# An attention, Fourier-mixing and MLP kernel: model-dimension tables from row-shift matmuls, a scale read from PSUM, fold work on GpSimd, and clock-keeping matmuls

## The chip, the cores and the metric

The kernel runs on one core of one Trainium2 chip. The metric is the device time of one execution, in microseconds (us). A time is "of an execution"; a span is the stretch from the first to the last instruction in the profile, about 2 us shorter. Executions of one kernel differ by 1 to 2%, and those more than 1.5% above the fastest of the same kernel are called slow and left out of ratios.

The engines are named as the profile names them: PE is TensorE's matmul, PEld its weight load, DVE is VectorE, ACT is ScalarE, POOL is GpSimd and SP is SyncE. On this kernel SP issues the input loads, and POOL issues the weight loads.

## The reference, cut to what matters

```python
B, H, S, D = 4, 8, 768, 48                    # r, k, v, w: (B, H, S, D); u: (H, D)
for t in range(S):                            # attention with a decaying state
    cur   = k_t^T v_t * u
    y_t   = r_t (state + cur)
    state = w_t * state + k_t^T v_t
x = y.transpose(0, 2, 1, 3).reshape(4, 768, 384)
mixed = real(fft(fft(x, axis=1), axis=2))     # over the sequence, then over the model dimension
u  = x + mixed
un = (u - mean(u)) / sqrt(var(u) + 1e-6)
out = u + relu(un @ w_ch1) @ w_ch2            # (384 x 1536), (1536 x 384)
```

## The kernel before

Every batch passes through three stages. Attention takes 768 tokens as six chunks of 128 and gives `x`. The mix multiplies `x` with cosine and sine tables: first the sequence tables `CS` and `SS`, then the model-dimension tables `DTM` and `DTP`, which gives `uf = x + mixed`. The MLP multiplies with `W1` and `W2`. The kernel computes its tables itself, at the start.

The program is a list of operations. Each names its engine, an estimated duration, what it reads and writes, and a key. A greedy list scheduler in the kernel runs over it once, before launch, and fixes the order on every engine: at each step it takes the operation that can start first, and the one with the lowest key where several can. So nine numbers, from which most keys are made, and the estimated durations decide the order of everything. On the chip each engine then works through its own list in that order.

```python
# --- tables (cut): angles on VectorE, sine on ScalarE
for q in range(NC // 2):                      # 3 sequence tables: 4 VectorE operations each
    ...                                       # TF[q], TG[q]: angles
    sins.append(act(SS[:, q, :], TF[q][:, :], ACTF.Sin, scale=sc))
    sins.append(act(CS[:, q, :], TG[q][:, :], ACTF.Sin, scale=-sc, bias=BHPI[:, :]))
...                                           # 16 one-column operations on VectorE: MC, MN, MSH, MB, CP
for j in range(3):                            # 3 model-dimension tables, again 4 VectorE operations each
    ...
    op("dve", 550, stt(f, ki, MC[:, j:j + 1], q, ALU.mult, ALU.add), ...)
    sins.append(act(DTM[:, j, :], f, ACTF.Sin, scale=sc2, bias=MB[:, j:j + 1]))
op("act", 8000, all_sins, ...)                # one operation for all nine Sins: needs ALL angles
...
# --- weights: 6 loads issued by GpSimd, held back until the third chunk's v has landed
op("pool", 1000, lambda e, q=q: e.dma_start(W1[:, q, :], moe_w_ch1[...]), r=[("in", "v", 2)], ...)
...
# --- attention(b, c): one chunk (cut)
op("act", 500, act(L[:, :, 0:D], wt[:, :, :], ACTF.Ln), ...)                    # lb
op("act", 470, act_ps(e1, tce), r=[tce], w=[("E1", i2)])                        # exp, PSUM -> SBUF
op("pool", 1050, tt(rk[:, :, :], rt[:, :, :], kt[:, :, :], ALU.mult), ...)
op("act", 500, act(vb[:, :, :], vt[:, :, :], ACTF.Copy), ...)                   # vb: v in bf16
op("dve", 700, tt(rh[:, :, 0:D], rt[:, :, :], e1[:, :, :], ALU.mult), ...)      # rh = r * exp
...                                           # transposes, rtb, ktb, masked products ah, state, y
op("dve", 530, ...)                                                             # x = y + vtd
op("dve", 350, tt(xf[:, c, 64:256],  xb[:, c, 0:192], xb[:, c, 384:192:-1], ALU.add), ...)       # even fold
op("dve", 350, tt(xf[:, c, 256:447], xb[:, c, 1:192], xb[:, c, 383:192:-1], ALU.subtract), ...)  # odd fold
# --- mix(b) (cut)
op("act", 475, ...)                                                             # hcs, from the sequence transform
op("dve", 390, lambda e, j=j: e.tensor_copy(out=hcr[:, j, :], in_=hcs[:, j, S // 2:0:-1]), ...)
...                                           # uf, statistics
op("dve", 100, ts(nmu[:, :], agg[:, kb, 0:1], -1.0, None, ALU.mult), ...)
op("act", 600, act(un[:, :], uf[:, kb, :], ACTF.Identity, bias=nmu[:, :]), ...) # un = u - mean
...                                           # transposes of un; W1: 288 matmuls; W2: 288 matmuls
A0, AP, F0, FL, M0, ML, P, KT, KW = 39.3, 5.6, 23.3, 16.1, 48.9, 42.4, 44.9, 7.9, 13.3
```

## Time and profile before

| | before |
|---|---|
| time, median of 3 (range) | 237.49 us (236.5 to 238.16) |
| span of the profiled run | 235.8 us |
| first W1 matmul | 72.24 us |
| VectorE busy before it | 66.64 of 72.24 us |
| PE busy after it | 156.74 of 163.56 us |

First, the page of the kernel before. The first line is the busy time of each engine with its share of the span. The others cut the span into 40 slices of 5.9 us; each digit is the busy share of one slice in tenths, and `PEclk` is the granted clock of the tensor engine in tenths of full speed.

```profile
PE 200.0 (85%) x1776; PEld 130.1 (55%) x1776; DVE 185.5 (79%) x403; ACT 153.1 (65%) x316; POOL 105.0 (45%) x118
PE   0765475549769999999998999899989999999994
DVE  8999999398998389999769998894899866822222
PEclk9998555577995999999999999999999999999999
DMA  6999999989970559852365678104200000020102
```

Read the rows against each other. In the first twelve slices most of PE's digits are 4 to 7, its clock is at 5 or 7 in six of them, and VectorE and DMA have mostly nines. From then on nearly all of PE's digits are nines. So there are two stages, and the mean share of PE, 85%, describes neither.

The next view is the busy time of each engine in two stretches of the kernel before, cut at the first W1 matmul. The columns are the stretch, its length, then busy time and number of instructions of PE, PEld, DVE, ACT and POOL, then mean granted clock, DMA share and GB/s.

```profile
0.00:72.24 72.24, 43.25 (x362) 27.72 (x363) 66.64 (x149) 42.01 (x79) 47.93 (x60) 0.77 0.99 186
72.24:235.80 163.56, 156.74 (x1416) 102.41 (x1414) 118.88 (x255) 111.12 (x238) 57.09 (x58) 0.99 0.34 80
```

In the first stretch VectorE (66.64 of 72.24) and DMA (share 0.99) are full, and PE is not. In the second, PE is busy 156.74 of 163.56 us.

The chain of waits of the kernel before, followed back from the last instruction, has these pieces among others. The columns are start, length in us, and what it was; L389 is a helper for activations, L620 is `x`, and L708 is W1.

```profile
24.82 16.01 DMA in_v<-in_v_dram
...
40.85 0.52 ACT vb L389
...
57.79 0.47 DVE x L620
...
72.45 0.96 PE bank L708 x3
```

The last chunk's `v` lands at 40.83 us, but the last `x` of batch 0 starts 17 us later, and W1 another 15 us later. What lies between is shown by the timeline of the kernel before (start, length, engine, line, operation, output and inputs):

```profile
38.42 0.60 DVE L383 SCALAR_TENSOR_TENSOR ht<-ki,mc,tq 128x384 f32<-128x384 f32 x1
...
44.88 0.53 ACT L389 ACTIVATE ss<-uf 128x385 bf16<-128x385 f32 x1
...
48.67 0.60 ACT L389 ACTIVATE dtm<-ht,mb 128x384 bf16<-128x384 f32 x1
...
57.72 0.54 DVE L620 TENSOR_TENSOR x<-bank,vtd 128x384 f32<-128x384 f32 x1
...
64.80 1.01 DVE L666 TENSOR_TENSOR uf<-bank,x 128x384 f32<-128x384 f32 x2
```

The first line is the last of the table angles, on VectorE at 38.42 us. The Sins wait for it and for their turn, so they run to 49.3 us.

Next are two of the three forms of `rh` in the kernel before, which differ only in the buffer. The numbers are the shortest, median and longest duration in ns, then the first and last start.

```profile
L375 DVE TENSOR_TENSOR rh<-in_r,e_0 x8: 525/554/1370, 7.1 to 177.0; 128x384 bf16<-128x384 f32 x8
L375 DVE TENSOR_TENSOR rh<-in_r,e_1 x8: 548/1158/1347, 13.7 to 180.4; 128x384 bf16<-128x384 f32 x8
```

The same operation on the same shape takes about 0.55 us or, in ten of all 24, 0.99 to 1.37 us, which is the sign of something that blocks it at times. The trace shows what it is: each of the ten starts while a multiplication on GpSimd is under way, and ends 0.41 to 0.43 us after that one ends. Of the fourteen short ones only two start during one, in its last 0.16 us.

Last, waits of the kernel before in the stretch after the first W1 matmul: who waited for what, us in total, times, longest.

```profile
PEld bank L648 <- DVE xf L375: 2.8, 6, 1.0
...
PE bank L648 <- DVE xf L375: 1.0, 2, 0.6
...
PE bank L612 <- DVE ah L587: 0.9, 1, 0.9
PE bank L564 <- DVE rh L375: 0.9, 1, 0.9
```

### The profile page before, as it was taken

The numbers are of one execution on the slowest core, as the hardware profiler recorded it, in microseconds if no ns is written. First come the engines' busy times: TensorE is split into PE (matmuls) and PEld (weight loads), VectorE is DVE, ScalarE is ACT, GpSimd is POOL, SyncE is SP. The second block draws the span as 40 slices with busy tenths as digits, with TensorE's granted clock in tenths as the row PEclk, the third lists the DMA queues.
The fourth block names the chain that finished last, engine by engine and source line by source line (L and its number), as shares of the span: only waits on it lengthen the run. The fifth ranks groups of instructions, "written<-read, shape, count | busy, mean of one in ns | idle before, by whom it ended". The sixth has DMA issues, their size and how long they took to land.

```text
span 235.8 us, 4671 instructions
## 1 busy us (share of the span) xinstructions
PE 200.0 (85%) x1776; PEld 130.1 (55%) x1776; DVE 185.5 (79%) x403; ACT 153.1 (65%) x316; POOL 105.0 (45%) x118
## 2 busy tenths in 40 slices
PE   0765475549769999999998999899989999999994
PEld 0443253436335575666776766467757765666652
DVE  8999999398998389999769998894899866822222
ACT  3554542997466997566887977488969554965340
POOL 7587894629901589282165965401633100000000
PEclk9998555577995999999999999999999999999999
DMA  6999999989970559852365678104200000020102
GB/s 120 211 213 219 183 189 197 214 176 216 198 143 3 100 104 211 191 117 52 81 155 104 133 156 181 38 0 110 60 0 3 36 33 33 3 101 0 70 33 100
DMA packets 105478, 26.45 MB, mean 112 GB/s; under 512 B 100336, under 2 KB 105072, under 8 KB 105456
## 3 DMA queue, kind: packets, MB, share of 16 engines
q1 hardware_dynamic: 103440, 23.80, 47.5%
q0 software_dynamic: 2016, 2.36, 5.9%
q8 instruction: 14, 0.23, 0.4%
q14 instruction: 8, 0.07, 0.1%
HBM read 23.79 MB, written 4.72 MB: 121 GB/s over the span
## 4 chain that ended last, share of the span: by engine, by line
PE 63%; DVE 19%; DMA 9%; ACT 5%; issue 2%; SPq 1%; DVEq 0%; ACTq 0%
PE bank L727 19%; PE bank L708 18%; DMA in_v<-in_v_dram 7%; DVE xf L375 6%; PE bank L648 6%; PE bank L664 5%; PE bank L564 3%; PE bank L583 3%; DVE rh L375 3%; DVE ah L587 3%; DVE x L620 2%; PE bank L684 2%; DMA in_w<-in_w_dram 2%; PE bank L612 2%; PE bank L570 1%
## 5 line engine op out<-in xcount | busy, mean ns | idle before, releaser
L708 PE MATMUL bank<-unt,w 128*128 128x384 bf16 x288 | 58.0, 333 | 0.0
L727 PE MATMUL bank<-w,ht 128*128 128x384 bf16 x288 | 54.1, 326 | 0.0
L717 ACT ACTIVATE ht<-bank 128x384 bf16<-128x384 f32 x80 | 37.9, 500 | 19.2 <-PE bank L708 19.0
L587 DVE TENSOR_TENSOR ah<-bank,msk 128x512 bf16<-128x512 f32 x48 | 31.1, 679 | 8.2 <-PE bank L583 8.1
L375 POOL TENSOR_TENSOR vtd<-in_v,dc 128x384 f32<-128x384 f32 x24 | 21.1, 884 | 35.8 <-DVE dc L545 32.7
L708 PEld LDWEIGHTS bank<-unt,w 128*128 128x128 bf16 x288 | 26.9, 99 | 16.1 <-issue 1.0
L727 PEld LDWEIGHTS bank<-w,ht 128*128 128x128 bf16 x288 | 26.9, 98 | 15.3
L573 ACT ACTIVATE rtb<-bank 128x1024 bf16<-128x1024 bf16 x24 | 24.6, 1025 | 15.0 <-PE bank L564 14.8
L732 DVE SCALAR_TENSOR_TENSOR osb<-bank,rstd,uf 128x384 f32<-128x384 f32 x24 | 14.8, 615 | 17.2 <-PE bank L727 16.7
L375 DVE TENSOR_TENSOR xf<-x 128x192 bf16<-128x192 f32 (+1 forms) x48 | 26.6, 593 | 0.1
L375 POOL TENSOR_TENSOR rk<-rk,ub 128x384 f32<-128x384 f32 x24 | 25.2, 1051 | 1.3
L375 POOL TENSOR_TENSOR rk<-in_r,in_k 128x384 f32<-128x384 f32 x24 | 25.4, 1060 | 0.0
L564 PE MATMUL bank<-idb,rh 128*128 128x128 bf16 x192 | 17.2, 242 | 8.7 <-DVE rh L375 8.1
L375 POOL TENSOR_TENSOR kh<-in_k,e_0 128x384 bf16<-128x384 f32 x8 | 8.8, 1096 | 31.3 <-ACT e_0 L538 31.3
L575 ACT ACTIVATE ktb<-bank 128x512 bf16<-128x512 bf16 x24 | 14.3, 597 | 9.5 <-PE bank L570 9.3
L564 PEld LDWEIGHTS bank<-idb,rh 128*128 128x128 bf16 x192 | 13.7, 108 | 11.8 <-DVE rh L375 8.5
L612 PE MATMUL bank<-vb,ah 128*128 128x48 bf16 x192 | 15.8, 189 | 5.0 <-DVE ah L587 4.9
L583 PE MATMUL bank<-rtb,ktb 128*128 128x256 bf16 x96 | 17.4, 309 | 1.8 <-ACT rtb L573 1.1
L525 PE MATMUL bank<-lb,msk 128*128 128x384 bf16 x24 | 9.4, 391 | 11.1 <-ACT lb L389 11.1
L713 DVE TENSOR_SCALAR ht<-bank 128x384 bf16<-128x384 f32 x16 | 8.8, 552 | 12.6 <-PE bank L708 12.6
L612 PEld LDWEIGHTS bank<-vb,ah 128*128 128x128 bf16 x192 | 13.1, 100 | 9.5 <-DVE ah L587 6.5
L389 ACT ACTIVATE lb<-in_w 128x384 bf16<-128x384 f32 x24 | 12.5, 523 | 5.9 <-DMA in_w<-in_w_dram 5.9
(111 smaller groups left out, 403.1 us busy)
## 6 DMA issues: line engine op xcount, KB each, us to landing
in_w<-in_w_dram SPq DMA_DIRECT2D x24, 192.0 KB, 3.7
in_k<-in_k_dram SPq DMA_DIRECT2D x24, 192.0 KB, 3.7
in_r<-in_r_dram SPq DMA_DIRECT2D x24, 192.0 KB, 3.7
in_v<-in_v_dram SPq DMA_DIRECT2D x24, 192.0 KB, 3.5
out_dram<-osb SPq DMA_DIRECT2D x24, 192.0 KB, 1.9
w<-in_moe_w_ch_dram POOLq DMA_DIRECT2D x6, 384.0 KB, 9.7
ub<-in_u_dram SPq DMA_DIRECT2D x1, 192.0 KB, 3.8
```

Source lines behind the costliest of these rows:

```text
L375: return lambda e: e.tensor_tensor(out=o, in0=a, in1=b, op=f)
L564: ins = e.transpose(psb(trr)[:, 128 * h:128 * h + 128], rflat[:, o0:o0 + 128], IDB[:, :])
L573: op("act", 1000, lambda e: e.activation(rT[:, :, :].rearrange("p h t -> p (h t)"), psb(trr)[:, :], ACTF.Copy), r=[trr], w=[("RTB", i2)])
L575: op("act", 570, lambda e: e.activation(kT[:, :, :].rearrange("p h t -> p (h t)"), psb(trk)[:, 0:512], ACTF.Copy), r=[trk], w=[("KTB", i2)])
L583: ins = e.matmul(ps(ta)[:, 256 * x:256 * x + 256], kT[:, q, :], rT[:, 2 * q:2 * q + 2, :].rearrange("p h t -> p (h t)"))
L587: op("dve", 660, lambda e, hf=hf, ta=ta: e.tensor_tensor(out=ah[:, 4 * hf:4 * hf + 4, :], in0=ps(ta)[:, :].rearrange("p (h t) -> p h t", t ...
L612: ins = e.matmul(ps(ty)[:, D * h:D * h + D], ah[:, h, :], vb[:, h, :], start=True, stop=first)
L648: return e.matmul(ps(t)[:, 0:HF], xf[:, s, off:off + 128], tab[:, s, :], start=a, stop=z)
L708: ins = e.matmul(ps(t)[:, 0:384], W1[:, m, 128 * j:128 * j + 128], unt[:, m, :], start=(m == 0), stop=(m == NM - 1))
L717: op("act", 475, lambda e, j=j, t=t, ht=ht: e.activation(ht[:, j, :], ps(t)[:, 0:384], ACTF.Relu), r=[t], w=[("HT", q % 2, j)])
L727: ins = e.matmul(ps(t)[:, 0:DM], ht[:, j, 128 * x:128 * x + 128], W2[:, j, :], start=(j == 0), stop=(j == NJ - 1))
L732: op("dve", 540, lambda e, kb=kb, t=t, o=o: e.scalar_tensor_tensor(out=o[:, :], in0=ps(t)[:, 0:DM], scalar=rstd[:, kb:kb + 1], in1=uf[:, k ...
```

## The change

The intent is to take work off VectorE in the first stage, to have the tables early, and to keep the tensor engine's clock up while it is poorly fed.

1. The model-dimension tables are rows of the sequence tables in another order, because 768 is twice 384. 14 small matmuls with shifted identities (`IDW`, `NIDW`) pick these rows out of `CS` and `SS` into PSUM, and ScalarE copies them to `DTM` and `DTP`. Their angles, three Sins and the 16 one-column operations go (two new ones make `CP`).
2. The exponential that scales `r` is written in place in PSUM, and `rh` reads it there.
3. The odd fold of batches 1 to 3 and the reversed copy `hcr` go from VectorE to GpSimd; the `ALT` vector too.
4. `un` becomes mean minus u, and its transposes use the negative identity, so `nmu` goes.
5. 24 pairs of matmuls into a bank that nobody reads are strewn over the first stage, to keep the clock up.
6. All nine numbers of the keys are chosen anew; the tables get first priority (`KT` 0.0).
7. Estimated durations of operations that stay are changed too (the even fold from 350 to 520 ns, `vtd` from 1050 to 890, `osb` from 540 to 610, the angles of the sequence tables), and with them the order.

```diff
-        op("dve", 350, ts(ALT[:, :], TQ[1][:, :], -2.0, 1.0, ALU.mult, ALU.add), ...)     # and 4 before it
+        op("pool", 300, fill(ALT[:, :], 1.0), w=["ALT0"])
+        op("pool", 200, fill(ALT[:, 1::2], -1.0), r=["ALT0"], w=["ALT"])
 ...
-        op("dve", 100, ts(IS1[:, :], p, 62.5, None, ALU.is_gt), ...)                      # and 15 like it
-        for j in range(3):
-            ...                                                                           # 4 VectorE operations
-            sins.append(act(DTM[:, j, :], f, ACTF.Sin, scale=sc2, bias=MB[:, j:j + 1]))
+        for j in range(3):
+            def rows(e, j=j, t=t):
+                for half in range(2):
+                    for i, (cos, q, p0, np_, sh) in enumerate(moves[j]):
+                        tab = (CS if cos else SS)[p0:p0 + np_, q, :]
+                        idn = (IDW if cos or half else NIDW)[p0:p0 + np_, 128 - sh:256 - sh]
+                        src = tab[:, 0:HF:2] if half == 0 else tab[:, HF - 3:0:-2]
+                        ins = e.matmul(dst, idn, src, start=(i == 0), stop=(i == len(moves[j]) - 1))
+            op("pe", 600, rows, ...)
+            op("act", 475, ... e.activation(DTM[:, j, :], ps(t)[:, 0:DM], ACTF.Copy) ...)
+            op("act", 475 + 100, ... e.activation(DTP[:, j, :], ps(t)[:, 0:DM], ACTF.Copy, scale=...) ...)
 ...
-        op("act", 470, act_ps(e1, tce), r=[tce], w=[("E1", i2)])
+        op("act", 470, lambda e: e.activation(ps(tce)[:, 0:DM], ps(tce)[:, 0:DM], ACTF.Exp), w=[tce])
 ...
-        op("dve", 700, tt(rh[:, :, 0:D], rt[:, :, :], e1[:, :, :], ALU.mult), ...)
+        op("dve", 550, lambda e: e.tensor_tensor(out=rh[:, :, 0:D], in0=ps(tce)..., in1=rt[:, :, :], op=ALU.mult), ...)
 ...
-        op("dve", 350, tt(xf[:, c, 256:447], xb[:, c, 1:192], xb[:, c, 383:192:-1], ALU.subtract), ...)
+        op("dve" if b == 0 else "pool", ..., tt(xf[:, c, 256:447], ...), ...)
 ...
-            op("dve", 390, lambda e, j=j: e.tensor_copy(out=hcr[:, j, :], in_=hcs[:, j, S // 2:0:-1]), ...)
+            op("pool", 500, lambda e, j=j: e.tensor_copy(out=hcr[:, j, :], in_=hcs[:, j, S // 2:0:-1]), ...)
 ...
-    A0, AP, F0, FL, M0, ML, P, KT, KW = 39.3, 5.6, 23.3, 16.1, 48.9, 42.4, 44.9, 7.9, 13.3
+    W0, WP, NW = 8.0, 1.6, 24
+    A0, AP, F0, FL, M0, ML, P, KT, KW = 46.4, 4.2, 24.5, 13.8, 48.1, 44.3, 45.6, 0.0, 0.5
 ...
+    for i in range(NW):
+        def warm(e):
+            for x in range(2):
+                ins = e.matmul(ps(tw)[:, 0:384], MSK[:, :], IDW[:, :])
+            return ins
+        o = op("pe", 324, warm, r=["MSK", "IDB"], w=[tw], key=1e6)
+        o.ready0 = 1e3 * (W0 + WP * i)
```

## The prediction

> **What bounds it now.** Two phases. From 72.45 us (first W1 matmul, in the chain of waits) to the end at 235.8 the tensor engine is busy 156.5 of 163.4 us at clock 0.99 (busy time by windows), and the chain runs almost only through its matmuls: PE-bound. Before 72.45 the PE's mean clock is 0.77 and it often waits. There VectorE is the limit: busy without a gap from 0.9 to 41 us (timeline), since tables and attention of batch 0 share it. The Sin calls run only at 43.6-49.3 us, batch 0's last `x` at 57.7, its first `uf` at 64.8. DMA is the other limit: share 1.0 or more from 10 to 50 us at about 200 GB/s; chunk 5's `v` lands at 40.85.
>
> **What the change does.**
> - Removes from VectorE before the first mix: the `alt` chain (2.7 us), about 20 one-column operations (about 3), DTM angles (7.7), DTP (1.6): about 14 us with overlaps taken off (groups by line). Adds about 0.8 for wider identities. 14 row-shift matmuls (0.16-0.2 us each) and six 0.5 us PSUM copies on ScalarE replace three 0.6 us Sins.
> - The table gets first priority: in the instruction order all angles precede the first `ah`, and the Sins follow chunk 2's exponential. I expect Sins at 15-22 us.
> - `rh` reads its scale from PSUM: 24 at mean 0.84 us become about 0.55. Now they are 0.55 unblocked, 1.16-1.37 blocked. The Trainium skill, "SBUF — State Buffer", "Who interferes with whom", says a VectorE instruction with two SBUF inputs contends with a GpSimd one that reads SBUF, and with one it does not; the two clusters agree.
> - Per later batch VectorE loses six odd-half `xf` (0.55), three `hcr` (0.52), six `nmu` (0.14): about 6 us; GpSimd gains as much, to 31 of 45 us. Slack of a PE-bound stage: worth 0-2 us.
> - 48 clock-keeping matmuls, 8-16 us of PE time, all before the first W1 matmul, mostly in idle gaps. They should hold the clock near 1 at 24-60 us, where it is 0.5-0.7 now ("TensorE: Matmul & The Clock Gate", Part 1: the clock falls after an idle window and returns after sustained activity).
>
> **Sum.** From instruction counts times full-clock durations (0.163 us for 384 columns), PE work after the first W1 matmul is 152 us before, 153 after: an estimate. So the time moves by the start of that phase. VectorE's work up to the first `uf`, unblocked, is about 41 us after (about 60 now). DMA still delivers chunk 5 no sooner than 36-41 us; then 5-6 us to `x`, 4-5 to `uf`, 6-7 to W1 (7.6 now, at a reduced clock). First W1 matmul: 57 us (52-63) instead of 72.5. The later phase keeps its 163 us, less 1-2 for a clock that no longer dips (0.70 at 72-80), plus 1 for work moved. 57 + 163 + 1.7 (time above span) = 222 us.
>
> **Right if:** first W1 matmul at 52-63; VectorE has gaps before 41 us, waiting for DMA; Sins before 23 us; `rh` mean 0.55; clock at least 0.9 in 10-60 us; second phase 160-165 us; first-phase DMA share still about 1.
>
> **Wrong if:** the weights, now issued at about 15 us, take bandwidth from chunks 3-5, so batch 0 ends past 50 us; the Sins stall chunks 1-2; GpSimd's odd-half folds queue behind `rk`/`vtd` and starve the mix later; warm matmuls, in order, sit before urgent ones. These push toward 230. Batch 0 flowing at DMA speed pushes toward 214.
>
> Predicted 222 us, range 214-230; faster by over 2%: 0.91, within 2%: 0.07, slower: 0.02.

## The result, and the profile after

In its first four executions the changed kernel took 223.81 us (median; 220.48 to 224.77) against 237.0 (236.3 to 238.16), a ratio of fast runs of 0.9349 [0.9237, 0.946]; two of the four, at 224.75 and 224.77, count as slow. Its profiled execution was a slow one, so the kernel was run and profiled again with five rounds: 223.03 us (220.36 to 223.25, six executions), against 237.15 (235.15 to 237.85) for the kernel before in the same rounds. That ratio is 0.9392 [0.9345, 0.9438], or 6% faster. A ratio is the mean time of one kernel's fast runs over that of the other's in the same rounds, so it is not quite the ratio of the medians that are quoted. The profile below is the one of the repeated run, which was fast; it is used for all comparisons.

> The changed kernel once more, in the rounds that the next kernels share, because its profiled run fell in the slower state. Expected: 218 to 223 us, ratio to before 0.93 to 0.945, first W1 matmul at 62 to 65 us, the stretch after it 156 to 160 us long.

The page of the changed kernel (slices of 5.5 us):

```profile
PE 199.4 (90%) x1838; PEld 130.6 (59%) x1838; DVE 156.6 (71%) x316; ACT 151.4 (69%) x319; POOL 118.7 (54%) x150
PE   0687586989799999999999999999999999999994
DVE  8998955994975797859678976783997839522322
PEclk9999958999969999999999999999999999999999
DMA  5999999999994979951254993015001010111102
```

VectorE has 29 us less work in all, PE's is the same although it has 62 more matmuls, and the clock row has lost its fives but one.

The two stretches of the changed kernel, cut at its first W1 matmul (columns as above):

```profile
0.00:61.65 61.65, 43.65 (x406) 26.95 (x407) 51.98 (x104) 40.60 (x78) 45.66 (x62) 0.94 1.04 195
61.65:220.60 158.95, 155.72 (x1432) 103.67 (x1432) 104.57 (x213) 110.77 (x242) 73.06 (x89) 0.99 0.39 91
```

The first stretch is 10.6 us shorter, and the second 4.6 us. The DMA share of the first has gone up to 1.04, VectorE's load has come down to 51.98 of 61.65 us.

The chain of waits of the changed kernel from 17 to 66 us (L384 is the activation helper, L370 the helper of `xf`, L649 is `uf`, L688 is W1):

```profile
18.70 17.23 DMA in_v<-in_v_dram
...
35.96 0.52 ACT vb L384
...
37.52 2.12 DVE xf L370 x2
...
54.66 1.02 DVE uf L649 x2
...
61.65 0.83 PE bank L688 x3
```

Here the chain again passes a load of `v`, but it is the fifth chunk's and not the last one's. It is issued at 18.70 us, amid the six weight loads that GpSimd issues from 17.2 to 21.2 us, and lands 17.2 us later; the median load of `v` in this run takes 3.6. The last chunk's `v` is issued only at 38.33 us, and lands at 42.01. The same thing was in the kernel before, with the weights issued from 22.6 us on and the last chunk's `v`, issued at 24.82, taking 16.0 us; there VectorE was late anyway. From that landing on, the chain of the changed kernel is VectorE and PE work without a large wait.

The timeline of the changed kernel (the lines of POOL issue the weight loads):

```profile
17.15 1.82 POOL L488 DMA_DIRECT2D w<-in_moe_w_ch_dram  x3
17.20 0.53 ACT L384 ACTIVATE ss<-uf 128x385 bf16<-128x385 f32 x1
...
18.94 2.27 POOL L491 DMA_DIRECT2D w<-in_moe_w_ch_dram  x3
...
19.47 0.60 ACT L384 ACTIVATE cs<-ht,bhpi 128x385 bf16<-128x385 f32 x1
...
49.79 0.56 DVE L606 TENSOR_TENSOR x<-bank,vtd 128x384 f32<-128x384 f32 x1
...
54.66 1.02 DVE L649 TENSOR_TENSOR uf<-bank,x 128x384 f32<-128x384 f32 x2 [2.85 <-PE bank L647]
```

The six remaining Sins are done at 20.1 us instead of 49.3. The last `x` of batch 0 starts at 49.79 instead of 57.72, and `uf` at 54.66 instead of 64.80; before `uf` VectorE is now idle for 2.85 us, where it had no gap before.

`rh` in the changed kernel:

```profile
L538 DVE TENSOR_TENSOR rh<-bank,in_r x24: 538/547/559, 8.5 to 171.1; 128x384 bf16<-128x384 f32 x24
```

All 24 are short. The Trainium skill, "SBUF — State Buffer", section "Who interferes with whom", says that a VectorE instruction with two SBUF inputs contends with a GpSimd one that reads SBUF, and that with one SBUF input it does not; the one that comes second waits in full. The slow ones of 0.99 to 1.37 us, each of which outlasted a GpSimd instruction that had started first, are gone once one input comes from PSUM.

PE's waits in the second stretch of the changed kernel. There are no lines of `PE` any more, only of `PEld`, and these are the two largest:

```profile
PEld bank L688 <- issue: 0.9, 5, 0.3
PEld bank L569 <- ACT ktb L561: 0.6, 2, 0.4
```

### Where the 15.2 us of span come from

From the number and width of the matmuls in a stretch and their durations at full clock (0.163 us for 384 columns, 0.109 for 256, 0.057 for 128, 0.043 for 96, 0.025 for 48), PE's work after the first W1 matmul is an estimate of 152.1 us before and 153.3 after. So the span is start + work + rest:

| | first W1 matmul | PE work after it (estimate) | rest | span |
|---|---|---|---|---|
| before | 72.24 | 152.1 | 11.5 | 235.8 |
| after | 61.65 | 153.3 | 5.65 | 220.6 |
| difference | -10.6 | +1.2 | -5.85 | -15.2 |

The rest falls into PE's idle time, 163.56 - 156.74 = 6.8 us before and 158.95 - 155.72 = 3.2 after, and into busy time above the estimate, 4.6 and 2.4. In the first 7.8 us after the start the clock was 0.70 before and 0.78 after, so some 0.6 us (7.8 x 0.08) of the second part is clock, by estimate; what the other 1.6 us are was not found.

### The profile page after: what moved, and what is told of

Its sections match the earlier page's. It is cut to its first block, busy times and chain, and to the rows that moved or that the text cites. A ratio compares the mean times of both kernels' runs of the same rounds, so it can differ in the third digit from the quotient of the medians.

```text
span 222.5 us, 4731 instructions
## 1 busy us (share of the span) xinstructions
PE 198.4 (89%) x1838; PEld 130.2 (59%) x1838; DVE 157.4 (71%) x316; ACT 151.2 (68%) x319; POOL 118.8 (53%) x150
## 3 DMA queue, kind: packets, MB, share of 16 engines
q0 software_dynamic: 2016, 2.36, 6.3%
## 4 chain that ended last, share of the span: by engine, by line
PE 75%; DMA 8%; SPq 8%; DVE 4%; ACT 3%; issue 1%; DVEq 0%
PE bank L688 22%; PE bank L707 21%; DMA in_v<-in_v_dram 8%; SPq L393 8%; PE bank L631 7%; PE bank L647 4%; PE bank L550 4%; PE bank L569 4%; PE bank L598 2%; PE bank L556 2%; PE bank L664 2%; PE bank L601 2%; PE bank L510 1%; PE bank L512 1%; DVE xf L370 1%; PE bank L586 1%
## 5 line engine op out<-in xcount | busy, mean ns | idle before, releaser
L688 PE MATMUL bank<-unt,w 128*128 128x384 bf16 x288 | 56.9, 330 | 0.2
L688 PEld LDWEIGHTS bank<-unt,w 128*128 128x128 bf16 x288 | 26.6, 99 | 15.9 <-issue 1.1
L370 POOL TENSOR_TENSOR rk<-in_r,in_k 128x384 f32<-128x384 f32 x24 | 25.0, 1040 | 5.6 <-DMA in_k<-in_k_dram 3.7
L370 POOL TENSOR_TENSOR rk<-rk,ub 128x384 f32<-128x384 f32 x24 | 24.9, 1036 | 0.8
L370 POOL TENSOR_TENSOR vtd<-in_v,dc 128x384 f32<-128x384 f32 x24 | 21.0, 880 | 6.5 <-DVE dc L530 6.5
L550 PE MATMUL bank<-idw,rh 128*128 128x128 bf16 x192 | 15.5, 226 | 4.7 <-ACT lb L384 3.3
L693 DVE TENSOR_SCALAR ht<-bank 128x384 bf16<-128x384 f32 x16 | 8.9, 555 | 14.4 <-PE bank L688 14.4
L370 POOL TENSOR_TENSOR xf<-x 128x191 bf16<-128x191 f32 x18 | 11.2, 622 | 13.7 <-DVE x L606 13.7
L370 DVE TENSOR_TENSOR xf<-x 128x192 bf16<-128x192 f32 (+1 forms) x30 | 17.7, 606 | 0.1
L649 DVE TENSOR_TENSOR uf<-bank,x 128x384 f32<-128x384 f32 x24 | 12.3, 541 | 7.7 <-PE bank L647 7.7
L538 DVE TENSOR_TENSOR rh<-bank,in_r 128x384 bf16<-128x384 f32 x24 | 13.2, 549 | 5.9 <-ACT bank L514 5.9
L550 PEld LDWEIGHTS bank<-idw,rh 128*128 128x128 bf16 x192 | 12.6, 101 | 8.0 <-ACT e_1 L523 3.4
L598 PE MATMUL bank<-vb,ah 128*128 128x48 bf16 x192 | 15.0, 186 | 2.0 <-DVE ah L573 1.8
L606 DVE TENSOR_TENSOR x<-bank,vtd 128x384 f32<-128x384 f32 x24 | 13.3, 556 | 4.7 <-PE bank L601 4.5
L384 ACT ACTIVATE vb<-in_v 128x384 bf16<-128x384 f32 x24 | 12.7, 531 | 5.4 <-DMA in_v<-in_v_dram 5.4
```

Source lines behind the costliest of these rows:

```text
L370: return lambda e: e.tensor_tensor(out=o, in0=a, in1=b, op=f)
L550: ins = e.transpose(psb(trr)[:, 128 * h:128 * h + 128], rflat[:, o0:o0 + 128], IDB[:, :])
L598: ins = e.matmul(ps(ty)[:, D * h:D * h + D], ah[:, h, :], vb[:, h, :], start=True, stop=first)
L688: ins = e.matmul(ps(t)[:, 0:384], W1[:, m, 128 * j:128 * j + 128], unt[:, m, :], start=(m == 0), stop=(m == NM - 1))
```

## The experiments

The theory was this: the start of the MLP moved because the tables are early and VectorE has less to do, and it is 4.7 us later than predicted because the early weight loads delay batch 0's `v`. The rivals were that the clock-keeping matmuls or the new nine numbers do it, and that the second stretch gained by VectorE's relief there.

All runs gave a correct result. Ratios are to the kernel before of the same rounds. All profiles of runs 1 to 10 are of fast runs.

| run | edit to the changed kernel | time, median (range), us | ratio to before [95%] | first W1 | rest |
|---|---|---|---|---|---|
| after again | none | 223.03 (220.36-223.25) | 0.9392 [0.9345, 0.9438] | 61.65 | 5.65 |
| 1 no warm | no clock-keeping matmuls | 225.16 (223.93-227.03) | 0.9519 [0.9472, 0.9566] | 62.56 | 5.8 |
| 2 weights late | weights after the last `v` of batch 0 | 223.59 (221.44-224.13) | 0.942 [0.9376, 0.9464] | 66.39 | 3.7 |
| 3 old tables | tables as before | 231.05 (230.08-231.66) | 0.9748 [0.971, 0.9786] | 73.05 | 4.85 |
| 4 rh from SBUF | scale in SBUF again | 227.23 (226.0-229.46) | 0.9616 [0.9566, 0.9665] | 66.49 | 5.0 |
| 5 fold on VectorE | odd folds and `hcr` on VectorE | 227.96 (227.62-228.69) | 0.9627 [0.9595, 0.9658] | 64.62 | 8.3 |
| 6 old numbers | the nine numbers of before | 228.96 (228.66-229.46) | 0.9669 [0.9638, 0.97] | 69.65 | 5.65 |
| 7 before, new numbers | kernel before with the nine new ones | 241.64 (240.74-244.09) | 1.0212 [1.0164, 1.026] | 76.13 | 12.3 |
| 8 late, retuned | run 2, one copy less, numbers re-chosen | 219.99 (218.03-221.71) | 0.9248 [0.9198, 0.9299] | 62.75 | 3.45 |
| 9 fifth, retuned | weights after the fifth `v`, else like 8 | 223.79 (221.1-224.06) | 0.9412 [0.9363, 0.9462] | 65.95 | 3.85 |
| 10 double warm | 96 instead of 48 clock-keeping matmuls | 223.1 (222.65-223.93) | 0.941 [0.9374, 0.9446] | 63.28 | 4.2 |

Only runs 1 and 10 keep the order of every engine, because there the matmuls were taken out, or doubled, after the scheduler had run. In run 5 the order before the first W1 matmul is that of the changed kernel except for `hcr`. In all others the scheduler makes a new order, and an edit's cost includes that of its order.

Two cautions for the last two columns. They do not add up to the span, because the order also decides how much of PE's work comes after the first W1 matmul: by the same estimate 151.1 us (run 3) to 153.3. And each run has one profile, while the start differs between profiles of one kernel: the slow profile of the changed kernel has the first W1 matmul at 63.68 us and a rest of 5.5, and run 11, which is the kernel of run 1 again, has 65.22 and 5.7. So a start that differs by less than about 2.7 us shows nothing by itself; the rest repeats within 0.3 us. The profiles of runs 1 and 4 are of their fastest executions, that of run 8 is of one of its slower ones.

### Run 1: without the clock-keeping matmuls

```diff
+    # after g.schedule(): leave out the 24 operations and hand their dependences on
+    g.order["pe"] = [o for o in g.order["pe"] if o not in ws]
```

> The changed kernel without its 48 clock-keeping matmuls, all other instructions in the same order on every engine. My theory (the earlier start comes from VectorE being rid of the table work, held back by the loads): the granted clock over 10 to 60 us falls to 0.75 to 0.85, but the first W1 matmul stays at 63 to 67 us and the time within 2 us of the changed kernel. Rival (the start is early because the clock is kept up): the first W1 matmul moves to 69 us or later and the time to 228 us or more.

It took 225.16 us, 1.3% of the kernel before's time more than the changed kernel, or 3.0 us ((0.9519 - 0.9392) x 237); the intervals do not overlap. So the 48 matmuls are worth about 3 us. But the clock did not fall to 0.75 to 0.85, as was expected. Here is the stretch from 10 to 60 us (the clock is the third number from the end) of the kernel before, then of run 1:

```profile
10.00:60.00 50.00, 31.22 (x271) 20.49 (x272) 45.38 (x86) 30.35 (x57) 36.15 (x38) 0.69 1.08 200
```

```profile
10.00:60.00 50.00, 37.16 (x327) 22.99 (x325) 40.57 (x73) 33.93 (x65) 35.09 (x40) 0.93 1.08 199
```

With them it is also 0.93 in the profiled execution of the changed kernel. But a profile is one execution, and that of the kernel before has one of its low clocks. In the 33 executions of the kernel before beside runs 1 to 10 the mean clock over the span goes from 0.913 to 0.986, and is 0.951 in the mean; it is 0.967 in run 1 and 0.983 in the changed kernel. So about half of the rise of this mean is there without the matmuls.

The time does not follow this clock. The ten executions of the kernel before at 0.984 or more have a mean span of 235.3 us, and the thirteen at 0.934 or less one of 235.2. In run 1, an execution at 0.977 has a span of 224.0 us and one at 0.939 has 223.2. This speaks against the clock as the way in which the 48 matmuls gain 3 us; what the way is was not found.

### Run 10: twice as many

```diff
-            for x in range(2):
+            for x in range(4):
```

> The changed kernel with 96 instead of 48 clock-keeping matmuls, same order. Without them the time rose by 1.3 percent, though the profiled clock over 10 to 60 us was about the same (0.9). If they act through the clock and more activity is better: mean granted clock of the runs at 0.985 or more, time 219 to 223 us. If they delay the real matmuls behind them as much as they help: 223.5 to 227 us with the clock not higher.

It took 223.1 us; its ratio, 0.941, is within the interval of the changed kernel. The clock did go up, from 0.93 to 0.97 between 10 and 60 us, and all six executions have a mean clock of 0.992 over the span. It bought nothing: the first W1 matmul came 1.6 us later, which is within what two profiles of one kernel differ by, and the rest was 1.4 us shorter.

```profile
10.00:60.00 50.00, 44.97 (x425) 29.12 (x422) 39.72 (x72) 33.54 (x65) 34.93 (x40) 0.97 1.06 196
```

### Run 11: another look without them

> A second profile of the kernel without clock-keeping matmuls, because the first profile was of the fastest of its six executions (span 221.7 us against 222.3 to 224.8) and does not show where the 1.3 percent went. If the half clock lengthens the chain of batch 0: first W1 matmul at 63.5 to 65.5 us and clock in 10 to 60 us under 0.9. If it lengthens the start of the stretch after it: first W1 matmul at 62 to 63 us and that stretch 160 us or longer.

This was the kernel of run 1 again, in one execution of unknown state: 226.44 us, beside 236.82 of the kernel before. It was to show where the 3 us of run 1 are. The first W1 matmul came at 65.22, and the second stretch was the same 158.98 us. The clock was 0.74 and 0.75 from 30 to 40 and from 40 to 50 us (0.77 and 1.00 with the matmuls). But in this execution a load of `r` that was issued at 18.03 landed only at 36.36, and ScalarE waited 5.4 us for a `v` (4.5 in the changed kernel). So a lower clock and loads that happen to land later come together here, and how much of the 3 us is clock stays open. Both looks have a later start than the changed kernel's (by 0.9 us and 3.6), and neither shows a loss in the second stage; but the two profiles of the changed kernel itself differ by 2.0 us in the start, so that the loss lies there is not shown.

### Run 2: weights later

```diff
-               r=[("in", "v", 2)], w=[("W1", q)], ...
+               r=[("in", "v", 0)], w=[("W1", q)], ...        # the last v of batch 0; the same for W2
```

> The changed kernel with the six weight loads held until the last v of batch 0 has landed, instead of the third v. My theory (the weights took the bandwidth that chunks 3 to 5 needed, so v of the fifth chunk landed at 36.7 us and the first W1 matmul came 6.7 us later than predicted): that v lands by 28 us, the first W1 matmul starts at 54 to 58 us, time 212 to 217 us. Rival (VectorE's own work sets the start, the loads are covered): first W1 matmul at 61 us or later, time 219 to 223 us. Second risk: the weights land after 55 us and are waited for.

The wait for `v` is gone, as the theory said. The time did not fall: 223.59 us, ratio 0.942. The first W1 matmul came at 66.39, later than with the wait. Even the last `x` of batch 0 came no earlier, at 50.46 against 49.79, although the last two `v` of the batch had landed by 22.62 and 29.85. The first stretch of run 2:

```profile
0.00:66.39 66.39, 47.18 (x436) 28.91 (x437) 55.38 (x109) 44.45 (x85) 45.85 (x63) 0.92 1.05 197
```

And one of its waits between 15 and 66 us:

```profile
ACT lb L384 <- DMA in_w<-in_w_dram: 2.2, 1, 2.2
```

The first stretch now holds 30 more matmuls and seven more ScalarE instructions than that of the changed kernel: the scheduler put more of batch 1 ahead of batch 0's mix. ScalarE waited 2.2 us for the `w` of a later chunk, at 49.4 to 51.6 us, with copies that batch 0's mix needs behind it in its list. So the theory in its simple form, that the loads alone made the start late, fell: a wait went away and others came. The rival's expectation, a start at 61 us or later, is the one that held.

### Runs 8 and 9: weights later, with numbers that fit

```diff
-               r=[("in", "v", 2)], ...
+               r=[("in", "v", 0)], ...                       # run 9: ("in", "v", 4), the fifth v
+            if j == 0:
+                continue                                      # DTP's first plane equals DTM's: use that one
-    A0, AP, F0, FL, M0, ML, P, KT, KW = 46.4, 4.2, 24.5, 13.8, 48.1, 44.3, 45.6, 0.0, 0.5
+    A0, AP, F0, FL, M0, ML, P, KT, KW = 47.3, 4.5, 24.5, 14.0, 48.5, 40.4, 44.6, 0.0, 30.0
```

(Run 9 has ML = 44.4 and KW = 20.0 and keeps the other seven.)

> A try for a faster version: the weights after the last v of batch 0 as in the second experiment, one needless table copy dropped (the first plane of the mirrored table equals the unmirrored one), and the nine scheduling numbers chosen anew for this program. If the second experiment gained nothing only because its instruction order was made for early weights, so that ScalarE, in order, waited for loads of batch 1: no wait for a load over 2 us on ScalarE before the first W1 matmul, that matmul at 55 to 61 us, time 216 to 220 us. If the stretch before it is limited by VectorE and ScalarE work and the chain from chunk to chunk whatever the loads do: 221 to 224 us.

> The same with the weights held only until the fifth v (chunk 4) has landed, with scheduling numbers close to those of the changed kernel. As before: 217 to 221 us if the loads' order cost the 4 to 5 us that ScalarE waits for that v in the changed kernel, 221 to 224 us if that wait only hides other limits.

Run 8 took 219.99 us, ratio 0.9248 [0.9198, 0.9299]. It is faster than both kernels: by 7.5% than the kernel before, and by 3.4 us ((0.9392 - 0.9248) x 237) than the changed kernel, with intervals that do not overlap. Run 9 took 223.79 us and gained nothing. The stretches of run 8:

```profile
0.00:62.75 62.75, 44.12 (x417) 28.00 (x418) 51.84 (x108) 42.58 (x81) 47.71 (x64) 0.92 1.03 193
62.75:218.80 156.05, 152.59 (x1422) 102.52 (x1422) 101.50 (x210) 108.87 (x239) 71.40 (x86) 1.00 0.40 92
```

And two of its waits between 15 and 63 us:

```profile
DVE rh L540 <- DMA in_r<-in_r_dram: 5.5, 1, 5.5
...
ACT vb L384 <- DMA in_v<-in_v_dram: 4.6, 1, 4.6
```

The last `x` of batch 0 came at 45.24 us, against 49.79 in the changed kernel: with the weights issued from 32.3 us on and this order, batch 0 ends 4.5 us earlier. But the waits are now for batch 1's loads. VectorE's list holds an `rh` of batch 1 ahead of batch 0's `uf`, and VectorE waits for its `r` up to 53.30 us. So from the last `x` to W1 it takes 17.5 us (62.75 - 45.24) instead of 11.9, and W1 starts 1.1 us later than in the changed kernel. What made the profiled execution of run 8 faster (by 1.8 us of span, of the 3.4 in the mean) is elsewhere: the rest is 3.45 us instead of 5.65, and PE's work after the start is 152.6 instead of 153.3. Three edits were made together, and how much each of them gives was not separated. So the time fell into the range that was expected (216 to 220 us), but not for the reason: the start was to be at 55 to 61 us, with no wait of ScalarE for a load over 2 us.

### Run 3: the tables as before

```diff
-        (row-shift matmuls, copies to DTM and DTP, ALT on GpSimd)
+        (the tables of the kernel before: 9 Sins, angles and ALT on VectorE)
```

> The changed kernel with the model-dimension tables computed on VectorE as in the kernel before (and its alternating-sign vector), with the new priorities and everything else kept. My theory: about 13 us of VectorE work come back before the first mix, of which the gaps of about 9 us in the first 60 us hide a part: first W1 matmul at 68 to 74 us, time 226 to 231 us. Rival (the priority given to the tables is what helps, not the work removed): first W1 matmul within 2 us of the changed kernel, time within 2 us of it.

It took 231.05 us: 8.4 us more ((0.9748 - 0.9392) x 237), the largest loss of any part. VectorE's load in the first stretch went back to 66.34 us, which is that of the kernel before, and the first W1 matmul to 73.05, although the tables still had first priority. In this order the Sins ran at 34.8 to 39.2 us, so the run takes back the early tables together with VectorE's relief; which of the two makes how much of the later start was not separated. The first stretch of run 3:

```profile
0.00:73.05 73.05, 47.58 (x430) 29.52 (x431) 66.34 (x144) 44.12 (x83) 48.25 (x64) 0.93 1.02 192
```

Note the clock, 0.93 against 0.77 before in an equally long stretch, with the same load on VectorE: a clock that was held up did not shorten this stretch.

### Run 4: the scale through SBUF

```diff
-        op("act", 470, ... e.activation(ps(tce)[:, 0:DM], ps(tce)[:, 0:DM], ACTF.Exp), w=[tce])
+        op("act", 470, ... e.activation(E1[i2][:, :, :], ps(tce)..., ACTF.Exp), r=[tce], w=[("E1", i2)])
-        op("dve", 550, ... in0=ps(tce)..., in1=rt[:, :, :] ...)
+        op("dve", 700, tt(rh[:, :, 0:D], rt[:, :, :], E1[i2][:, :, :], ALU.mult), ...)
```

> The changed kernel with the receptance scale written to SBUF again and rh formed from two SBUF operands. Expected under my theory (a port shared with GpSimd costs rh its time, and only the stretch before the first W1 matmul is sensitive to VectorE): rh mean back at 0.75 to 0.95 us, first W1 matmul 1 to 3 us later than in the changed kernel, time 223 to 226 us. Rival: if rh is off the critical path everywhere, the mean rises and the time stays within 1 us; if VectorE bounds the steady stage after all, the time rises by 5 us or more.

It took 227.23 us, 5.3 us more. The group of `rh` in run 4 (count, then busy time in us and mean ns, then idle time before it):

```profile
L371 DVE TENSOR_TENSOR rh<-in_r,e 128x384 bf16<-128x384 f32 x24 | 18.7, 779 | 2.5 <-ACT e L515 2.5
```

The mean is 779 ns, with durations up to 1355, so the slow cluster is back. That is 5.6 us of VectorE time more (18.7 against 13.1) over the whole run. In the profiled execution, the fastest of the six, the span is 3.3 us longer, and the loss is in the start (66.49 against 61.65); the rest is 5.0 us. But blocking explains only a part of it. The last `x` of batch 0 comes at 55.40 us, 5.6 later, and the eight `rh` before it take 5.96 us, where eight short ones take 4.4: 1.6 us. The edit also makes a new order, in which eight `rh` come before that `x` (six in the changed kernel); later landings of `v` are not behind the other 4 us (the last two of batch 0 land 0.3 and 0.5 us earlier than in the changed kernel), but that the order is was not shown by itself.

### Run 5: odd folds and the reversed copy on VectorE

```diff
-        op("dve" if b == 0 else "pool", 600 if b == 0 else 750, tt(xf[:, c, 256:447], ...
+        op("dve", 600, tt(xf[:, c, 256:447], ...
-            op("pool", 500, lambda e, j=j: e.tensor_copy(out=hcr[:, j, :], ...
+            op("dve", 390, lambda e, j=j: e.tensor_copy(out=hcr[:, j, :], ...
```

> The changed kernel with the odd half of the fold and the reversed copy back on VectorE in all batches. Theory: after the first W1 matmul the tensor engine is busy without a gap, VectorE at 0.7 to 0.8, so 15 us of VectorE work more are hidden: time within 2 us of the changed kernel (221 to 225 us), tensor engine idle after the first W1 matmul under 2 us. Rival (the fold on GpSimd is what removed the tensor engine's gaps of the stage after it, 4.5 us of the gain): 226 us or more, with waits of the tensor engine on the fold.

It took 227.96 us, 5.6 us more, so the rival's expectation held and the theory's did not. Its second stretch:

```profile
64.62:226.20 161.58, 156.27 (x1433) 103.22 (x1432) 117.31 (x240) 110.15 (x242) 58.17 (x61) 0.99 0.38 87
```

And a wait in it:

```profile
PEld bank L598 <- DVE ah L573: 2.0, 5, 1.3
```

PE's work is the same, 153.3 us, the clock is the same, and PE's idle time is 5.3 us (161.58 - 156.27) instead of 3.2. PE waits for VectorE's `ah` again. This is the test of what the second stretch gained from: of the 5.85 us that the rest lost, 2.65 us (8.3 against 5.65) come from folds and reversed copies that left VectorE. The other 3.0 us of the span are in the start (64.62 against 61.65). Some 2 us of these are not the edit's: the last `x` of batch 0 came at 51.88 us in this profile, 2.1 later than in the changed kernel's although the order up to there is the same, and a slow profile of the changed kernel itself has it at 51.81.

### Runs 6 and 7: the nine numbers alone

```diff
-    A0, AP, F0, FL, M0, ML, P, KT, KW = 46.4, 4.2, 24.5, 13.8, 48.1, 44.3, 45.6, 0.0, 0.5
+    A0, AP, F0, FL, M0, ML, P, KT, KW = 39.3, 5.6, 23.3, 16.1, 48.9, 42.4, 44.9, 7.9, 13.3
```

Run 6 is this edit to the changed kernel; run 7 is the opposite edit to the kernel before.

> The changed kernel with the nine scheduling numbers of the kernel before (tables after the first chunks, weights less urgent). If the priority of the tables matters as much as their cheaper making: Sins at 25 us or later, first W1 matmul at 65 to 69 us, 225 to 229 us. If only the removed work matters: within 2 us of the changed kernel.

> The kernel before with only the nine scheduling numbers of the changed kernel. If the numbers alone bring much of the gain: 228 to 232 us. My theory: VectorE is full up to 41 us whatever the order, so the tables finish earlier but the chunks later: 233 to 237 us, first W1 matmul at 69 to 73 us.

The changed kernel loses 6.6 us with the old numbers, and the kernel before loses 5.0 us (2.1%) with the new ones. So the numbers are not better in themselves; each set fits its own program. Run 6 came out as its first expectation said, with a start 0.65 us past its range; run 7 missed both of its own, which had only gains or no change. With the old numbers, the other edits bring 7.8 us ((1 - 0.9669) x 237) of the 14.4. Run 7 also shows the second stretch with VectorE loaded and the clock at full speed, so that most of the rest is idle time. Its second stretch:

```profile
76.13:239.50 163.37, 153.98 (x1400) 100.89 (x1399) 120.69 (x254) 109.11 (x233) 54.74 (x56) 1.00 0.33 77
```

And two of the waits in it:

```profile
PEld bank L648 <- DVE xf L375: 3.1, 5, 1.0
...
PE bank L612 <- DVE ah L587: 2.8, 5, 1.0
```

PE is idle for 9.4 us (163.37 - 153.98) in a stretch that looks PE-bound by its share, and VectorE is what it waits for.

### The costs do not add

Undoing one part costs 3.0 (clock-keeping), 8.4 (tables), 5.3 (`rh`), 5.6 (fold and copy) and 6.6 us (numbers). That is 29 us, against a gain of 14.4 ((1 - 0.9392) x 237). In all of these runs but the first, the order that was chosen for all parts together goes with the part that is undone, which may be why the sum is so large; it was not separated. So none of these numbers is the share of its part.

## Why the prediction was right, point by point

The time was predicted as 222 us (214 to 230), and it is 223.03, or 223.81 in the first four executions. The mechanism held: the change acts by an earlier first W1 matmul, through a shorter VectorE list and early tables. But two terms of the sum were mis-sized, in opposite directions: 57 + 163 + 1.7 was predicted, where the chip gave 61.65 + 158.95 + 2.3. That the sum comes within 2 us of 222 is luck in this sense: +4.7 and -4.1 us nearly cancel.

- **VectorE bounds the first stage: right.** With the old tables the start is at 73.05 us again (run 3). In the changed kernel VectorE was busy 9.37 us of 10 to 20 and 6.37 of 30 to 40 us; before it was full in both.
- **Sins at 15 to 22 us: right,** 17.2 to 20.1. The row-shift matmuls took 0.25 us each, where 0.16 to 0.2 was said, and were over at 22 us.
- **`rh` at 0.55 us: right,** mean 0.547, none blocked. Run 4, without it, costs 5.3 us, in its profile all in the first stage; blocking accounts for 1.6 us of that, and what the rest is was not separated.
- **First W1 matmul at 57 us (52 to 63): inside the range, but 4.7 us later than the number.** The term that was mis-sized is "then 5-6 us to `x`" after a landing of chunk 5 at 36 to 41 us. Chunk 5 is the last one (the prediction counts from 0); its `v` landed at 42.01 us and the last `x` started at 49.79, 7.8 us later. The next terms, 4-5 us to `uf` and 6-7 to W1, were right (4.9 and 7.0). And the chain did not go through that load at all: it went through the `v` of the fifth chunk, which landed at 35.93, and from there it took 14 us, mostly of VectorE's work, to the last `x`. The prediction had named the delay of these loads among its risks ("the weights ... take bandwidth from chunks 3-5, so batch 0 ends past 50 us"), and did not put it in the sum. The Trainium skill, "DMA: Bandwidth & Descriptors", section "Issuing engines are not separate DMA queues", says that loads issued by different engines run on the same 16 DMA engines and interleave. The trace agrees: SyncE's load of `v` took 17.2 us with GpSimd's six weight loads in flight, 3.6 in the median, and 3.6 for the very same load in run 2, where the weights came later. It could have been counted: the six loads are 2.36 MB, 12 us at the 200 GB/s of the trace. But runs 2 and 9 show that moving those loads does not by itself bring the time back, and only run 8, with numbers chosen anew, gained.
- **The second stretch "keeps its 163 us", less 1 to 2 for the clock, plus 1 for moved work: wrong by 3 to 4 us.** It was to be 162 to 163 and took 158.95, below the 160 to 165 that were named as the test. The moved work was right (+1.2). The term that failed is "Slack of a PE-bound stage: worth 0-2 us", and the sum counted it as 0. PE's idle time there fell from 6.8 to 3.2 us. A stage in which PE is busy 96% still holds 4% of waits, and the waits for `xf`, `ah` and `rh` stood in the profile before. Run 5 puts the folds and copies back on VectorE, and PE's idle time goes to 5.3 us; in run 7 the stretch idles 9.4 us. And the clock did not stop dipping: the first 7.8 us of the stretch ran at 0.78, against 0.70 before.
- **The clock at 0.9 or more from 10 to 60 us: right in the mean (0.93), not in each part** (0.77 from 30 to 40), **and only in part for the reason that was given.** Without the clock-keeping matmuls it is 0.93 and 0.90 in two profiles (runs 1 and 11); over the span, the mean of all executions is 0.951 before, 0.967 without them and 0.983 with them. The Trainium skill, "TensorE: Matmul & The Clock Gate", Part 1, says that the clock halves after an idle window and comes back after sustained activity. The profiled execution of the kernel before fits this, with 0.50 to 0.68 in each 10 us from 20 to 60 us, where PE was poorly fed. But other executions of the same kernel, in the same time, had 0.985 over the span, so how PE is fed is not all that decides the clock.
- **What did not happen.** GpSimd's folds did not starve the mix: in the second stretch the largest waits of PE, shown above, are not for GpSimd, and no line of 0.3 us or more is. The Sins did not stall the attention by much (VectorE waited 0.74 us for the last of them), and the clock-keeping matmuls delay nothing much, although one pair (0.32 us) lies on the chain before `uf`.

What stays open: how the clock-keeping matmuls gain their 3 us, since the times do not follow the clock; how the gain of run 8 splits among its three edits; and 1.6 us of PE's busy time in the second stretch of the kernel before.

## What to carry to other kernels

When two engines are full in a stage, take work off the one that the chain runs through, and ask at once whom the transfers will then collide with: here earlier weight loads held back a `v` of batch 0 by some 14 us (17.2 against 3.6). What that cost was not shown: moving the loads alone gained nothing. A stage that is 96% busy on its bounding engine still has waits, and the view of waits tells what they are for; count them in microseconds before calling a relief elsewhere worthless. Where a scheduler fixes the order, an edit and the numbers that it was tuned with belong together: test each with the other's, and tune again before judging an edit.

## What the Trainium skill lacked or had wrong

- "TensorE: Matmul & The Clock Gate", section "Terms", takes the penalty of a low clock as throttled time x (1 - K/N). It lacks a condition. In the profiled execution of the kernel before, the low clock lies before the first W1 matmul (0.77 there, 0.99 after), where PE is not the bound. The ten executions of the kernel before at a mean clock of 0.984 or more have a mean span of 235.3 us, and the thirteen at 0.934 or less (0.922 in the mean) one of 235.2, where the formula would have them 15 us apart (235 x 0.063, an estimate); and raising it from 0.93 to 0.97 between 10 and 60 us (run 10) changed nothing (ratios 0.9392 and 0.941).
- The same page has nothing on what clock-keeping matmuls are worth: 48 of them gave 1.3% here (run 1), and 48 more gave nothing (run 10).
- "ScalarE: Activation LUTs", section "Step-by-step: what each stage is for", says that ScalarE writes PSUM faster than SBUF. No difference is seen here: the 128x384 exponential written in place in PSUM takes 497 ns in the mean of 24, and those of the same shape written to SBUF take 487 to 498 ns in the kernel before.
- "DMA: Bandwidth & Descriptors", section "Issuing engines are not separate DMA queues", says that loads interleave, but gives no figure for what that costs an urgent one: a 192 KB load took 17.2 us amid six 384 KB loads (16.0 in the kernel before), and 3.6 in the median.
